# A two-layer attention and SiLU kernel: later raw loads for thirteen weight pairs, a token norm on ScalarE, one subtraction for two

## The chip, the cores and the metric

The kernel runs on one core of a Trainium2 chip. The time is device microseconds of one execution, the median of several. PE stands for TensorE's matmuls, PEld for its weight loads, DVE for VectorE, ACT for ScalarE, POOL for GpSimd, SP for SyncE (DMA issues and transposes). All times of the trace come from one profiled execution.

## The reference

The input x is 2048 tokens of width D = 576, in fp32.

```
for layer in (1, 2):
    x = x + attention(layernorm(x), wqkv) @ wo      # 32 heads of 18, a token looks at 8 tokens, 2 apart, backwards
    x = x + silu(layernorm(x) @ w1) @ w2            # w1: 576 x 4608, w2: 4608 x 576
```

Both layers use the same weights. layernorm has no scale or shift: (x − mean) / sqrt(var + 1e-5).

## The kernel before, in words

The tokens are cut into four chunks of 512 (four tiles of 128 tokens each), and the work into eight stages s = 0 to 7, two layers of four chunks. In each stage a chunk goes through attention, `project(s)` (the product with wo and the addition to x), a norm, and the hidden layer with w1 and w2. fp32 accuracy comes from fp16: each operand is split into a high part (x in fp16) and a low part (what is left), and a product is three fp16 products.

**Order.** Nobody writes the order of the instructions by hand. Each step is declared with `op(engine, cost, function, reads, writes, priority, after=...)`, and a planner (`Plan.order`) simulates the engines with these costs and the slots of the buffers, and hands out, for each engine, a fixed order. `after` names steps that must be over first. A new wait or a new cost therefore moves steps on all engines from that place on. Each engine works through its list strictly in order.

**Hidden layer.** Stages 0 and 1 multiply plainly (`ffn`, first products L1385, second products L1345). Stages 2 to 7 (`ffn_pairs`) take two of the 36 blocks of w1's columns together, a pair q = 0 to 17, and need seven products instead of eight (P1 to P7, L1232). For these, w1 must be brought into seven sums and differences, split into high and low. `prepare(q)` (L1064 to L1106) does so for each pair: eight raw loads on POOL's queue (L1072 four times 128 KB, L1076 four times 64 KB) into one of two `wr` slots, four sums on DVE (L1083), high parts on ACT (L1091), low parts on DVE (L1098, four per pair), and two stores on POOL (L1103) to `wfs` in HBM. `load_wf` (L1108) fetches them on SP. All 18 `prepare` are declared behind stage 0, and run beside stages 0 to 2. L1353 evicts second products of the pairs.

**Projection.** `project(s)` makes, for each of four token tiles, the high part of the attention's output (`yh`, L898 on DVE) and the low part (L492), lets SP turn the tile by a DMA transpose (L509, `yo<-yh`; `yh` has two slots), multiplies it by wo on PE in two halves (L925, 14 matmuls each, into one of three PSUM banks misc and z, which L1385 and L1232 use too), and adds the halves to x on DVE (L927). The list `flipped` collects the transposes. The third chunk's projection is the one at 555 to 600 us, beside the hidden layer of stage 1. POOL also fetches keys, values and queries for the attention (`kvs`, L779, 1584 KB; `qts`, L781, 288 KB).

**Norm and forms.** `forms` (L1158 on) takes bn_stats of a stage's x, `newton` (L524) finds r = 1/sqrt(var + eps), four L1179 on DVE write (x − mean) · r, L1184 makes differences of these, and L1193 (ACT) and L1198 (DVE) split them; L1203 turns them. Six stages use it. In stages 6 and 7 `hidden_forms` (L1283) makes four forms of the hidden h for the second product too: h4 = h6 + h3, h5 = h4 − h0, h2 = h1 − h5, h6 = h0 − h6.

Of the kernel before, what the change touches and what calls it, by code (L numbers as in the profile page):

```python
# [13 lines left out]
AF = mybir.ActivationFunctionType  # L14
ALU = mybir.AluOpType
AX = mybir.AxisListType

P = 128
# [8 lines left out]
NJ = 4  # L27
# [14 lines left out]
NP = NFT // 2  # L42
# [4 lines left out]
W2N = 11  # L47
FAR = 6
PREP = 0.9
PS = 0.45  # L50
S2 = 2
TWICE = {6: 0, 7: 0}
# [227 lines left out]
def sliding_attention_silu_ffn(ctx: ExitStack, tc: tile.TileContext, x, wqkv, wo, w1, w2, out):  # L280
# [243 lines left out]
    def newton(st, mv, nt, on_act, unit, js=slice(0, NJ)):  # L524

        v, r, a, b = (T(nt)[:, i, js] for i in (0, 1, 3, 4))
        if on_act == 2:
            nc.vector.tensor_scalar(v, T(st)[:, js, 0, 1], 1.0 / D, EPS, op0=ALU.mult, op1=ALU.add)
        else:
            nc.vector.tensor_scalar(v, T(mv)[:, js, 1], EPS, None, op0=ALU.add)  # L530
        nc.vector.tensor_scalar(a.bitcast(I32), v.bitcast(I32), 1, None, op0=ALU.logical_shift_right)
        nc.vector.tensor_scalar(r.bitcast(I32), a.bitcast(I32), -1, 0x5F3759DF, op0=ALU.mult, op1=ALU.add)
        for s in (1.0, unit):

            nc.vector.tensor_tensor(a, r, r, op=ALU.mult)
            nc.vector.tensor_tensor(a, a, v, op=ALU.mult)
            nc.vector.tensor_scalar(b, a, 0.375 * s, -1.25 * s, op0=ALU.mult, op1=ALU.add)
            nc.vector.tensor_tensor(b, b, a, op=ALU.mult)
            nc.vector.scalar_tensor_tensor(r, b, 1.875 * s, r, op0=ALU.add, op1=ALU.mult)
        if on_act in (1, 3):  # L540
            nc.vector.tensor_scalar(T(nt)[:, 2, js], T(mv)[:, js, 0], -1.0, None, op0=ALU.mult)

# [518 lines left out]
            nc.vector.tensor_scalar(dz, r12.rearrange("p (q f) i -> p q f i", f=2)[:, :, 0, 0], 2.0 / LNX, None, op0=ALU.mult)  # L1061
        op("DVE", 1.0, fn, [("s12", f) for f in range(NFT)] + [("sh", 2, g) for g in range(len(G2))], ["wsc"], -0.5)

    def prepare(q, prio):  # L1064

        w, v = Buf("wr"), Buf("ws")

        def load():
            t = T(w)
            for h in range(2):  # L1070
                for k in range(2):
                    nc.gpsimd.dma_start(t[:, h:4:2, k, :], w1[h * KH + k * P:h * KH + (k + 1) * P, 2 * q * P:(2 * q + 2) * P].rearrange(  # L1072
                        "p (f c) -> p f c", f=2))
                for f in range(2):
                    v = w1[h * KH + 2 * P:(h + 1) * KH, (2 * q + f) * P:(2 * q + f + 1) * P]
                    nc.gpsimd.dma_start(t[:, h + 2 * f, 2, :], bass.AP(tensor=v.tensor, offset=v.offset, ap=[[0, 4], *v.ap]))  # L1076
        op("POOL", 4.8, load, ["wsc"], [w], prio, nbytes=P * 12 * P * 4, lanes=8)

        def sums():
            t, u = T(w), T(v)  # L1080
            for o, a, b, f in ((u[:, 0], t[:, 2], t[:, 3], ALU.add), (u[:, 1], u[:, 0], t[:, 0], ALU.subtract),
                               (t[:, 2], t[:, 0], t[:, 2], ALU.subtract), (u[:, 2], t[:, 1], u[:, 1], ALU.subtract)):
                nc.vector.tensor_tensor(o, a, b, op=f)  # L1083
        op("DVE", 2.0, sums, [w], [w, v], prio)
        for x, r0, r1, g in ((w, 0, 4, Buf("wg")), (v, 4, 7, Buf("wh"))):
            n = r1 - r0

            def hi(x=x, g=g):
                d, t = T(g), T(x)
                for k0, k1, c in ((0, 2, 0), (2, 3, 1)):  # L1090
                    nc.scalar.activation(d[:, :, k0:k1, :].rearrange("p a b c -> p a (b c)"),  # L1091
                                         t[:, :, k0:k1, :].rearrange("p a b c -> p a (b c)"), AF.Copy, scale=wsc[:, q, c:c + 1])
            op("ACT", 0.4 * n, hi, [x, "wsc"], [(g, 0)], prio)

            def lo(x=x, g=g):
                d, t = T(g), T(x)
                for o, k0, k1 in ((3, 0, 2), (2, 2, 3)):
                    nc.vector.scalar_tensor_tensor(  # L1098
                        d[:, :, o:o + k1 - k0, :].rearrange("p a b c -> p a (b c)"),
                        t[:, :, k0:k1, :].rearrange("p a b c -> p a (b c)"), wsc[:, q, 0:1],  # L1100
                        d[:, :, k0:k1, :].rearrange("p a b c -> p a (b c)"), op0=ALU.mult, op1=ALU.subtract)
            op("DVE", 0.43 * n, lo, [x, (g, 0)], [(g, 0)], prio)
            op("POOL", 0.57, lambda g=g, r0=r0, r1=r1: nc.gpsimd.dma_start(  # L1103
                wfs[q][:, r0 * KB:r1 * KB], T(g).rearrange("p i a b -> p (i a b)")), [(g, 0)], [("wfs", q, r0 // 4)], prio, nbytes=P * n * KB * 2)
# [51 lines left out]
    def forms(xs, prio, home=None, late=(), into=None):  # L1156

        st, mv, nt = Buf("st"), Buf("mv"), Buf("nt")  # L1158
        for j in range(NJ):
            def stats(j=j):  # L1160
                for h in range(2):
                    nc.vector.bn_stats(T(st)[:, j, h, :], T(xs[j])[:, h * KH:(h + 1) * KH])
                nc.vector.bn_aggr(T(mv)[:, j, :], T(st)[:, j])
            op("DVE", 0.99, stats, [xs[j]], [(st, j), (mv, j)], prio)
        op("DVE", 2.55, lambda: newton(st, mv, nt, False, LNX), [(st, j) for j in range(NJ)] + [(mv, j) for j in range(NJ)], [nt], prio)
        out, ys = {}, [Buf(home[0]), Buf(home[1])] if home else [Buf(into)] * 2

        def view(a, r):
            if home:
                return T(ys[a])[:, r]  # L1170
            if r > 3:
                return T(ys[a])[:, a, r - 4]
            return T(xs[a + 2 - r // 2 * 2])[:, r % 2 * KH:(r % 2 + 1) * KH]

        def key(a, r):
            return (ys[a], r) if home else (ys[a], a, r) if r > 3 else xs[a + 2 - r // 2 * 2]
        for a in range(2):
            for j, r in ((a + 2, 0), (a, 2)):
                op("DVE", 0.58, lambda a=a, j=j, r=r: nc.vector.tensor_scalar(  # L1179
                    T(ys[a])[:, r:r + 2, :].rearrange("p a b -> p (a b)") if home else T(xs[j]), T(xs[j]), T(mv)[:, j, 0:1], T(nt)[:, 1, j:j + 1],  # L1180
                    op0=ALU.subtract, op1=ALU.mult), [xs[j], (mv, j), nt], [key(a, r), key(a, r + 1)], prio)

            for o, u, v in ((4, 0, 2), (5, 1, 4), (6, 1, 0), (7, 3, 5)):
                op("DVE", 0.45, lambda a=a, o=o, u=u, v=v: nc.vector.tensor_tensor(view(a, o), view(a, u), view(a, v), op=ALU.subtract),  # L1184
                   [key(a, u), key(a, v)], [key(a, o)], prio, after=late)
        for n in P_ORDER:
            r, x = Y_ROW[n], Buf("xf")
            for a in range(2):
                f = Buf("yf")

                def hi(f=f, a=a, r=r):
                    d, y = T(f), view(a, r)
                    nc.scalar.activation(d[:, 0:KH], y, AF.Copy)  # L1193
                    nc.scalar.activation(d[:, KH:KH + 32], y[:, 2 * P:KH], AF.Copy)

                def lo(f=f, a=a, r=r):
                    d, y = T(f), view(a, r)
                    nc.vector.tensor_tensor(d[:, 3 * P:KB], y[:, 0:2 * P], d[:, 0:2 * P], op=ALU.subtract)  # L1198
                    nc.vector.tensor_tensor(d[:, KH + 32:3 * P].rearrange("p (a b) -> p a b", a=2), y[:, None, 2 * P:KH].to_broadcast([P, 2, 32]),
                                            d[:, None, 2 * P:KH].to_broadcast([P, 2, 32]), op=ALU.subtract)  # L1200
                op("ACT", 0.65, hi, [key(a, r)], [(f, 0)] if home else [(f, 0), (x, "hold", a)], prio)
                done = op("DVE", 0.64, lo, [key(a, r), (f, 0)], [(f, 1)], prio)
                op("SP", 1.34, lambda f=f, a=a, x=x: nc.sync.dma_start_transpose(T(x)[:, :, a * P:(a + 1) * P], T(f)),  # L1203
                   [(f, 0), (f, 1)], [(x, a)], prio, nbytes=P * KB * 4)
            out[n] = x
        formed.append(done)
        return out
# [74 lines left out]

    def hidden_forms(q, hq, h, pd):  # L1283

        for r, u, v, o in ((4, 6, 3, ALU.add), (5, 4, 0, ALU.subtract), (2, 1, 5, ALU.subtract), (6, 0, 6, ALU.subtract)):
            op("DVE", 0.42, lambda hq=hq, r=r, u=u, v=v, o=o: nc.vector.tensor_tensor(T(hq)[:, r], T(hq)[:, u], T(hq)[:, v], op=o),
               [(hq, u), (hq, v)], [(hq, r)], pd - 0.01)
        for r0, r1, sh in ((0, 3, shx), (3, 7, shy)):
            sc = sh[:, q:q + 1]
            m = (r1 - r0) * 2 * P  # L1290
# [243 lines left out]
    for s in range(NL * NC):  # L1534
# [3 lines left out]
        else:  # L1538
            ffn_pairs(s, XT[s], X[s], TWICE.get(s, len(G2)))
        if s == 0:  # L1540
            for q in range(NP):
                prepare(q, PREP)
        if s == 2:
            op("POOL", 0.55, lambda: nc.gpsimd.dma_start(wos, fl(T(WO))), [(WO, k) for k in range(10)], ["wos"], 2.0, nbytes=P * 20 * D, after=flipped[-1:])
# [1 line left out]
            layer_norm(X[s], AN[s + NC] + 0.0, None, False, own=True, keep=xn[s - 2])  # L1546
        if s < NC - 1:
            front(s + 1)
        if s == NC - 1:
            norm(NC)  # L1550
            attend(NC)
# [41 lines left out]
```

## Time and profile before

| | |
|---|---|
| median of 3 runs | 2123.3 us (2121.58 to 2124.65) |
| the profiled execution | 2119.38 us, span 2117.6 us |
| PE busy | 2088.3 us (99%), 16017 matmuls |
| DVE busy | 1754.9 us (83%) |
| ACT busy | 1025.8 us (48%) |
| POOL busy | 388.5 us (18%) |
| chain of waits | PE 87%, DVE 6%, DMA 4% |

The span is from the first to the last instruction; the execution has 1.8 us around it. "Busy" leaves out DMA issues on SP and semaphores. The chain of waits is followed back from the last instruction, at each step to what released it.

### The profile page before, as it was taken

Reading aid. Unit: us, or ns where it says so; the run is one execution under the profiler, and the core shown is the slowest. Engines: PE = TensorE matmul, PEld = TensorE weight load, DVE = VectorE, ACT = ScalarE, POOL = GpSimd, SP = SyncE. Lnnn points to the kernel's source line nnn. Section 1 sums busy time; section 2 is a strip of 40 time slices with the busy share of each in tenths; the row PEclk is TensorE's granted clock in tenths of the full one; section 3 lists DMA queues with packets and bytes.
Section 4 is the critical chain, followed back from the end, with each engine's and each line's share of the span. In section 5 each row is a group of like instructions: output and inputs, shape, how many; then the busy total and the mean of one; then the engine's idle time right before and its main releaser. Section 6 shows DMA issues by size and latency. Waiting matters only on the chain.

```text
span 2117.6 us, 41751 instructions
## 1 busy us (share of the span) xinstructions
PE 2088.3 (99%) x16017; PEld 1539.5 (73%) x16017; DVE 1754.9 (83%) x2861; ACT 1025.8 (48%) x1857; POOL 388.5 (18%) x628
## 2 busy tenths in 40 slices
PE   8999999999999999999999999999999999999999
PEld 4556556665566888877786777777788888888887
DVE  8899999999876998679997978986996748766665
ACT  7555787644345454434434433434444545444442
POOL 2133566343322232011111001001000000000000
PEclk9999999999999999999999999999999999999999
DMA  6477777687989889886677896786989999779772
GB/s 188 146 212 256 236 258 248 214 243 221 250 206 297 264 275 252 210 261 189 177 220 208 218 273 195 217 225 185 247 256 302 330 258 290 218 213 272 221 210 76
DMA packets 377632, 489.07 MB, mean 231 GB/s; under 512 B 150600, under 2 KB 300724, under 8 KB 373080
## 3 DMA queue, kind: packets, MB, share of 16 engines
q1 hardware_dynamic: 332456, 336.85, 56.9%
q0 software_dynamic: 42960, 148.45, 21.8%
q8 instruction: 125, 2.05, 0.4%
q10 hardware_dynamic: 2016, 1.11, 0.2%
q14 instruction: 75, 0.61, 0.1%
HBM read 350.96 MB, written 86.85 MB: 207 GB/s over the span
## 4 chain that ended last, share of the span: by engine, by line
PE 87%; DVE 6%; DMA 4%; ACT 1%; issue 1%; SPq 0%; POOL 0%; ACTq 0%; DVEq 0%
PE acc L1345 19%; PE z L1232 16%; PE misc L1232 10%; PE z L735 9%; PE acc L1322 9%; PE z L1385 7%; PE acc L1409 4%; PE misc L1345 4%; PE misc L735 3%; PE z L925 3%; PE misc L1385 2%; PE misc L925 1%; DMA kvs<-kvs 1%; DMA yo<-yh 1%; DVE prs L837 1%
## 5 line engine op out<-in xcount | busy, mean ns | idle before, releaser
L1232 PEld LDWEIGHTS <-w 128*128 128x128 f16 x5292 | 516.5, 98 | 74.5 <-issue 2.5
L1345 PE MATMUL acc<-w,h 128*128 128x320 f16 (+2 forms) x3780 | 548.2, 280 | 2.3 <-DVE x L1353 2.3
L1345 PEld LDWEIGHTS <-h 128*128 128x128 f16 x4320 | 407.6, 98 | 122.3 <-issue 3.3
L1232 PE MATMUL z<-xb,w 128*128 128x256 f16 x3213 | 405.0, 273 | 0.5 <-DVE wq L1239 0.5
L1232 PE MATMUL misc<-xb,w 128*128 128x256 f16 x2079 | 272.2, 273 | 1.1 <-DVE wq L1239 0.8
L735 PEld LDWEIGHTS <-xa 128*128 128x128 f16 x1344 | 130.8, 98 | 115.5 <-issue 6.7
L837 DVE TENSOR_TENSOR prs<-qts,kvs 128x2304 f32<-128x2304 f32 x64 | 163.4, 2554 | 18.8 <-DMA kvs<-kvs 17.0
L870 DVE TENSOR_TENSOR prs<-kvs,pe 128x1152 f32<-128x1152 f32 x128 | 170.3, 1352 | 1.0
L841 DVE TENSOR_REDUCE lg<-prs 128x128 f32<-128x2304 f32 x64 | 163.1, 2548 | 0.9
L735 PE MATMUL z<-wq,xa 128*128 128x432 f16 x840 | 160.2, 346 | 2.1 <-ACT h L748 2.1
L1345 PE MATMUL misc<-w,h 128*128 128x384 f16 x540 | 139.7, 326 | 0.0
L877 DVE TENSOR_TENSOR prs<-prs 128x1152 f32<-128x1152 f32 (+1 forms) x128 | 135.1, 1056 | 3.2
L1331 DVE SCALAR_TENSOR_TENSOR x<-acc,d2x,x 128x576 f32<-128x576 f32 (+1 forms) x85 | 68.7, 810 | 57.2 <-PE acc L1322 56.6
L1385 PEld LDWEIGHTS <-w 128*128 128x128 f16 x588 | 57.9, 99 | 74.2 <-issue 7.6
L1409 PE MATMUL acc<-w,h 128*128 128x288 f16 x864 | 108.4, 286 | 1.9 <-DVE h L1392 1.1
L1409 PEld LDWEIGHTS <-h 128*128 128x128 f16 x864 | 83.7, 98 | 25.2 <-DVE h L1392 1.4
L1385 PE MATMUL z<-xb,w 128*128 128x512 f16 x420 | 93.9, 379 | 0.7 <-DVE w L1011 0.6
L1385 PE MATMUL z<-xb,wq 128*128 128x512 f16 x420 | 92.8, 379 | 1.7 <-ACT h L1387 1.7
L1236 ACT ACTIVATE wq<-z 128x256 f32<-128x256 f32 x107 | 40.8, 382 | 103.8 <-PE z L1232 103.7
L1387 ACT ACTIVATE h<-z,d 128x512 f32<-128x512 f32 x60 | 40.9, 682 | 94.9 <-PE z L1385 86.4
L1322 PEld LDWEIGHTS <-h 128*128 128x128 f16 x756 | 74.0, 98 | 17.6
L925 PEld LDWEIGHTS <-yo 128*128 128x128 f16 x672 | 65.7, 98 | 18.6 <-issue 1.9
(322 smaller groups left out, 3369.0 us busy)
## 6 DMA issues: line engine op xcount, KB each, us to landing
w<-wfs SPq DMA_DIRECT2D x756, 160.0 KB, 3.9
w<-w2s SPq DMA_DIRECT2D x180, 288.0 KB, 4.9
wq<-wqs SPq DMA_DIRECT2D x17, 1080.0 KB, 6.6
kvs<-kd POOLq DMA_DIRECT2D x8, 1584.0 KB, 8.4
w<-w1s SPq DMA_DIRECT2D x36, 320.0 KB, 5.9
wfs<-xa POOLq DMA_DIRECT2D x18, 640.0 KB, 4.6
kvs<-wts SPq DMA_DIRECT2D x80, 144.0 KB, 3.1
w2s<-w POOLq DMA_DIRECT2D x36, 288.0 KB, 4.7
```

The source lines that it names most:

```text
L735: nc.tensor.matmul(T(m)[:, :3 * UC], a, b, start=n == 0, stop=n == len(pl) - 1)
L837: nc.vector.tensor_tensor(T(pr), T(qt)[:, j:j + 2, None, :].to_broadcast([P, 2, W, UC]), win(T(kv), j, 2), op=ALU.mult)
L841: nc.vector.tensor_reduce(T(lg)[:, j:j + 2].rearrange("p a w h -> p (a w h)"), T(pr).rearrange("p a w (h d) -> p (a w h) d", d=DH), axis=A ...
L870: nc.vector.tensor_tensor(T(pr)[:, a].rearrange("p w (h d) -> p w h d", d=DH), v, T(pe)[:, j + a, :, :, None].to_broadcast([P, W, UH, DH]) ...
L877: nc.vector.tensor_tensor(t[:, :, 0:h, :], t[:, :, 0:h, :], t[:, :, h:2 * h, :], op=ALU.add)
L925: nc.tensor.matmul(T(m)[:, 0:288], a, b, start=n == 0, stop=n == len(pl) - 1)
L1232: nc.tensor.matmul(t, w[:, u, :], v[:, r, :], start=first and m == 0, stop=m == 6, skip_group_check=True)
L1322: nc.tensor.matmul(T(acc)[:, j, 0:KH], T(hb[t])[:, a, row[k], j * P:(j + 1) * P], T(wb[k, t])[:, w, :], start=k in (5, 1, 2) and t == 0 an ...
L1331: nc.vector.scalar_tensor_tensor(v, T(acc)[:, a:b, 0:KH], d2x[:, g:g + 1], v, op0=ALU.mult, op1=ALU.add)
L1345: nc.tensor.matmul(T(fa[b])[:, o:o + 2 * n].rearrange("p (a b) -> p a b", a=2), h(f, a, j), w(f)[:, :, v, c:c + n], start=q == f == m == 0 ...
L1385: nc.tensor.matmul(T(z), v, u, start=m == 0, stop=m == len(pl) - 1)
L1409: nc.tensor.matmul(T(acc)[:, h, 0:288], T(hb[q])[:, a, j * P:(j + 1) * P], T(wbs[q][0])[:, h, w, :], start=q == 0 and m == 0, stop=q == n ...
```

## The change

1. `prepare` of pairs 5 to 17 (HELD = 5 and on) is declared later, behind the third chunk's attention and projection, and its raw loads wait for the last entry of `flipped`, which is the transpose of the fourth tile of that projection.
2. In `forms`, the four normalisations of a stage go from DVE to ACT, as an Identity activation with scale r and bias −mean · r.
3. For these, `newton` gets one more 128x4 DVE operation (−mean · r), six times in all.
4. In `hidden_forms`, h5 = h4 − h0 and h6 = h0 − h6 become one DVE operation of 512 columns; the order is h4, then these, then h2.

```diff
+HELD = 5
...
+        if on_act == 4:
+            nc.vector.scalar_tensor_tensor(T(nt)[:, 2, js], T(mv)[:, js, 0], -1.0, r, op0=ALU.mult, op1=ALU.mult)
...
-    def prepare(q, prio):
+    def prepare(q, prio, after=()):
...
-        op("POOL", 4.8, load, ["wsc"], [w], prio, nbytes=P * 12 * P * 4, lanes=8)
+        op("POOL", 4.8, load, ["wsc"], [w], prio, nbytes=P * 12 * P * 4, lanes=8, after=after)
...
-        op("DVE", 2.55, lambda: newton(st, mv, nt, False, LNX), [(st, j) for j in range(NJ)] + [(mv, j) for j in range(NJ)], [nt], prio)
+        op("DVE", 2.55, lambda: newton(st, mv, nt, 4, LNX), [(st, j) for j in range(NJ)] + [(mv, j) for j in range(NJ)], [nt], prio)
...
-                op("DVE", 0.58, lambda a=a, j=j, r=r: nc.vector.tensor_scalar(
-                    T(ys[a])[:, r:r + 2, :].rearrange("p a b -> p (a b)") if home else T(xs[j]), T(xs[j]), T(mv)[:, j, 0:1], T(nt)[:, 1, j:j + 1],
-                    op0=ALU.subtract, op1=ALU.mult), [xs[j], (mv, j), nt], [key(a, r), key(a, r + 1)], prio)
+                op("ACT", 0.7, lambda a=a, j=j, r=r: nc.scalar.activation(
+                    T(ys[a])[:, r:r + 2, :].rearrange("p a b -> p (a b)") if home else T(xs[j]), T(xs[j]), AF.Identity,
+                    bias=T(nt)[:, 2, j:j + 1], scale=T(nt)[:, 1, j:j + 1]), [xs[j], (mv, j), nt], [key(a, r), key(a, r + 1)], prio)
...
-        for r, u, v, o in ((4, 6, 3, ALU.add), (5, 4, 0, ALU.subtract), (2, 1, 5, ALU.subtract), (6, 0, 6, ALU.subtract)):
-            op("DVE", 0.42, lambda hq=hq, r=r, u=u, v=v, o=o: nc.vector.tensor_tensor(T(hq)[:, r], T(hq)[:, u], T(hq)[:, v], op=o),
-               [(hq, u), (hq, v)], [(hq, r)], pd - 0.01)
+        op("DVE", 0.42, lambda: nc.vector.tensor_tensor(T(hq)[:, 4], T(hq)[:, 6], T(hq)[:, 3], op=ALU.add),
+           [(hq, 6), (hq, 3)], [(hq, 4)], pd - 0.01)
+
+        def differences():
+            t = T(hq)
+            first = bass.AP(tensor=t.tensor, offset=t[:, 4].offset, ap=[t.ap[0], [-4 * 2 * P, 2], [1, 2 * P]])
+            nc.vector.tensor_tensor(t[:, 5:7], first, t[:, 0:7:6], op=ALU.subtract)
+        op("DVE", 0.69, differences, [(hq, 4), (hq, 0), (hq, 6)], [(hq, 5), (hq, 6)], pd - 0.01)
+        op("DVE", 0.42, lambda: nc.vector.tensor_tensor(T(hq)[:, 2], T(hq)[:, 1], T(hq)[:, 5], op=ALU.subtract),
+           [(hq, 1), (hq, 5)], [(hq, 2)], pd - 0.01)
...
         if s == 0:
-            for q in range(NP):
+            for q in range(HELD):
                 prepare(q, PREP)
...
         if s < NC - 1:
             front(s + 1)
+        if s == 1:
+            for q in range(HELD, NP):
+                prepare(q, PREP, flipped[-1:])
```

The planner places everything anew from about 536 us on. The lines of the changed kernel are 3 higher up to L1284 (10 and more behind it).

SP's order around the third chunk's transposes, before. w_70 and w_87 are w1 and w2 blocks of stage 1's hidden layer, a pair of them per block.

```order
L941 DMA w_70<-w1s_166 128x1280
L509 DMA_TRANSPOSE yo<-yh 128x9x128
L946 DMA w_87<-w2s_199 128x1152
L941 DMA w_70<-w1s_167 128x1280
L509 DMA_TRANSPOSE yo<-yh 128x9x128 x2
L946 DMA w_87<-w2s_200 128x1152
L941 DMA w_70<-w1s_168 128x1280
L509 DMA_TRANSPOSE yo<-yh 128x9x128
```

And of the changed kernel:

```order
L944 DMA w_70<-w1s_164 128x1280
L510 DMA_TRANSPOSE yo<-yh 128x9x128 x2
L949 DMA w_87<-w2s_197 128x1152
L944 DMA w_70<-w1s_165 128x1280
L949 DMA w_87<-w2s_198 128x1152
L944 DMA w_70<-w1s_166 128x1280
L949 DMA w_87<-w2s_199 128x1152
L944 DMA w_70<-w1s_167 128x1280
L510 DMA_TRANSPOSE yo<-yh 128x9x128 x2
```

The first two transposes now go out together, two blocks earlier, and the last two together, three blocks behind them.

POOL's order at the same place, before. The raw loads (L1072, L1076) behind the second kvs fetch are those of pairs 6 and 7; wfs_219 to wfs_221 are the stores of pairs 5, 6 and 7.

```order
L1103 DMA wfs_219<-xa 128x2560
L1103 DMA wfs_219<-xa 128x1920
L779 DMA kvs<-kd_276 128x3168
L781 DMA qts<-qd_268 128x576
L1072 DMA wq<-in_B_w_dram 128x2x128 x2
L1076 DMA wq<-in_B_w_dram 128x1x128 x2
...
L1103 DMA wfs_220<-xa 128x2560
L1103 DMA wfs_220<-xa 128x1920
L1544 DMA wosd<-wos 128x5760
L1103 DMA wfs_221<-xa 128x2560
```

And of the changed kernel, in which the first loads behind the fetch are those of pairs 5 and 6, and wait for the fourth tile's transpose:

```order
L1106 DMA wfs_218<-xa 128x2560
L1106 DMA wfs_218<-xa 128x1920
L782 DMA kvs<-kd_276 128x3168
L784 DMA qts<-qd_268 128x576
L1075 DMA wq<-in_B_w_dram 128x2x128 x2
L1079 DMA wq<-in_B_w_dram 128x1x128 x2
...
L1106 DMA wfs_219<-xa 128x2560
L1106 DMA wfs_219<-xa 128x1920
L1554 DMA wosd<-wos 128x5760
L1106 DMA wfs_220<-xa 128x2560
```

POOL's work stands in the same order, one pair later, with the fetch of kvs and qts still ahead of the loads.

VectorE's order from the third of the projection's yh tiles on, before:

```order
L898 TENSOR_SCALAR yh<-o,so 128x576
L492 SCALAR_TENSOR_TENSOR yh<-o,so,yh 128x512
L492 SCALAR_TENSOR_TENSOR yh<-o,so,yh 128x64
L841 TENSOR_REDUCE lg_80<-prs 128x128
L898 TENSOR_SCALAR yh<-o,so 128x576
L927 SCALAR_TENSOR_TENSOR x_73<-misc_96,so,x_73 128x288
L492 SCALAR_TENSOR_TENSOR yh<-o,so,yh 128x512
```

And of the changed kernel:

```order
L901 TENSOR_SCALAR yh<-o,so 128x576
L493 SCALAR_TENSOR_TENSOR yh<-o,so,yh 128x512
L493 SCALAR_TENSOR_TENSOR yh<-o,so,yh 128x64
L901 TENSOR_SCALAR yh<-o,so 128x576
L493 SCALAR_TENSOR_TENSOR yh<-o,so,yh 128x512
L493 SCALAR_TENSOR_TENSOR yh<-o,so,yh 128x64
L844 TENSOR_REDUCE lg_80<-prs 128x128
L930 SCALAR_TENSOR_TENSOR x_73<-misc_96,so,x_73 128x288
```

The first eviction of the projection (L927, now L930) stands behind the fourth tile's yh in both; the fourth yh has moved up to the third.

## Rows read from the trace of the kernel before

**Rows 1.** The page, busy time of each engine with its share of the span and its number of instructions.
```profile
PE 2088.3 (99%) x16017; PEld 1539.5 (73%) x16017; DVE 1754.9 (83%) x2861; ACT 1025.8 (48%) x1857; POOL 388.5 (18%) x628
```
**Rows 2.** The waits of PE over the whole span, the first of the list: who waited for what, us in total, times, longest.
```profile
PE misc L1385 <- DVE x L927: 4.4, 1, 4.4
```
**Rows 3.** The waits of PE from 600 us to the end, all of the list; same columns.
```profile
PE acc L1345 <- DVE x L1353: 2.3, 5, 0.7
PE misc L925 <- DVE wq L1239: 1.8, 1, 1.8
PE misc L1232 <- DVE wq L1239: 0.8, 2, 0.5
PE z L1232 <- DVE wq L1239: 0.5, 1, 0.5
```
**Rows 4.** The chain of waits between 560 and 591 us: start, duration, what.
```profile
562.23 16.19 DMA yo<-yh
...
579.44 5.36 PE misc L1385 x14
...
588.24 3.02 PE misc L1385 x14
```
**Rows 5.** The timeline of DVE: start, duration (of all of a row together), engine, line, operation, tiles, count, and in brackets the idle time ahead and what ended it.
```profile
536.60 2.08 DVE L1083 TENSOR_TENSOR wq<-wq 128x384 f32<-128x384 f32 x4
...
544.87 3.40 DVE L1098 SCALAR_TENSOR_TENSOR xa<-wq,accw,xa 128x1024 f16<-128x1024 f32 x4
...
568.97 0.68 DVE L898 TENSOR_SCALAR yh<-o,so 128x576 f16<-128x576 f32 x1
...
578.44 0.52 DVE L898 TENSOR_SCALAR yh<-o,so 128x576 f16<-128x576 f32 x1 [5.35 <-DMA yo<-yh]
```
**Rows 6.** Windows: stretch, its length, busy time (and instructions) of PE, PEld, DVE, ACT and POOL, the granted clock as a share of full speed, the DMA engines' mean busy share, GB/s.
```profile
547.60:559.70 12.10, 12.10 (x58) 5.48 (x57) 11.93 (x17) 4.23 (x6) 5.99 (x10) 1.00 0.82 301
559.70:574.80 15.10, 15.10 (x125) 11.68 (x124) 13.28 (x11) 2.69 (x3) 7.21 (x10) 1.00 1.10 220
574.80:579.40 4.60, 0.26 (x3) 0.07 (x1) 0.96 (x3) 0.00 (x0) 0.00 (x0) 0.75 1.10 132
579.40:584.80 5.40, 5.36 (x16) 2.00 (x16) 5.23 (x13) 1.70 (x2) 0.00 (x0) 0.58 0.34 89
```
**Rows 7.** The timeline of SP's queue: transposes of the third and of the fourth chunk's projection; columns as in rows 5.
```profile
558.68 2.19 SPq L509 DMA_TRANSPOSE yo<-yh  x1
...
562.23 14.15 SPq L509 DMA_TRANSPOSE yo<-yh  x2
...
816.35 1.64 SPq L509 DMA_TRANSPOSE yo<-yh  x1
```
**Rows 8.** The timeline of POOL: the kvs fetch, the first and the last raw load of pairs 6 and 7, the first store of pair 6 and the last store of pair 17; columns as in rows 5.
```profile
554.21 0.54 POOL L779 DMA_DIRECT2D kvs<-kd  x1 [5.10 <-DVE prs L870]
...
555.27 1.43 POOL L1072 DMA_DIRECT2D wq<-in_B_w_dram  x2
...
573.80 0.70 POOL L1076 DMA_DIRECT2D wq<-in_B_w_dram  x1 [1.03 <-DMA wq<-in_B_w_dram]
591.87 0.58 POOL L1103 DMA_DIRECT2D wfs<-xa  x1 [17.36 <-DVE xa L1098]
...
845.94 0.54 POOL L1103 DMA_DIRECT2D wfs<-xa  x1 [4.25 <-DVE xa L1098]
```
**Rows 9.** The line L509 (all transposes of attention and projection): who waited for it (us, times), and the time from issue to landing.
```profile
  DVE yh L898: 5.4, 1
...
DMA to landing us min/median/max: 3.3/4.9/13.1
```
**Rows 10.** The timeline of PE: the first half of tile 0 of the fourth chunk's projection, the first product of pair 16 in stage 2 and that of pair 17; columns as in rows 5.
```profile
828.19 1.88 PE L925 MATMUL misc<-wos,yo 128*128 128x288 f16 x14
...
869.54 0.93 PE L1232 MATMUL misc<-xb,w 128*128 128x256 f16 x7
...
880.84 0.93 PE L1232 MATMUL z<-xb,w 128*128 128x256 f16 x7
```
**Rows 11.** The page's DMA issues: tiles, engine, count, KB each, median us from issue to landing.
```profile
w<-wfs SPq DMA_DIRECT2D x756, 160.0 KB, 3.9
...
kvs<-kd POOLq DMA_DIRECT2D x8, 1584.0 KB, 8.4
...
wfs<-xa POOLq DMA_DIRECT2D x18, 640.0 KB, 4.6
```
**Rows 12.** Groups of instructions by line over the whole span: line, engine, operation, tiles, shapes, count, busy us, mean ns of one, idle time ahead and what ended it. 16 of the 24 L1179 stand here, the other 8 have a mean of 578 to 602.
```profile
L1286 DVE TENSOR_TENSOR wq<-wq 128x256 f32<-128x256 f32 x96 | 38.6, 421 | 15.0 <-ACT wq L1261 10.2 <-ACT wq L1256 3.7
...
L591 ACT ACTIVATE yo<-x,nt 128x576 f32<-128x576 f32 x14 | 10.6, 767 | 4.1 <-DVE nt L541 2.3 <-DVE yh L492 1.6
L1179 DVE TENSOR_SCALAR x<-x,mv,nt 128x576 f32<-128x576 f32 x16 | 8.4, 574 | 0.0
...
L539 DVE SCALAR_TENSOR_TENSOR nt<-nt 128x4 f32<-128x4 f32 (+1 forms) x34 | 5.5, 162 | 1.2
```
**Rows 13.** Windows behind 600 us; columns as in rows 6.
```profile
600.00:860.00 260.00, 259.54 (x2063) 197.83 (x2061) 216.43 (x344) 124.06 (x215) 76.10 (x112) 1.00 0.90 262
860.00:1600.00 740.00, 735.80 (x5809) 559.30 (x5807) 632.27 (x974) 301.37 (x588) 72.03 (x124) 1.00 0.80 220
1600.00:2118.00 518.00, 512.54 (x4425) 430.48 (x4423) 345.61 (x633) 237.56 (x431) 12.90 (x24) 1.00 0.80 239
```

## The prediction

> **What bounds the kernel now.** I read the page first [rows 1]: PE is busy 99% of the span, VectorE 83%, ScalarE 48%. With PE that full, and the same 16017 matmuls after the change, a change of order can only give what PE loses by standing still or by running at a lower clock. So the second view is the list of PE's waits: one wait of 4.4 us is released by VectorE's L927, the longest single one of the run [rows 2]; after 600 us all waits together are 5.4 us [rows 3]. The third is the chain of waits around the long one [rows 4]. PE's first half of a hidden tile (L1385) waits for L927, the eviction of the third chunk's first projected half, because it needs that bank. L927 is ready long before, but on VectorE it stands behind the yh of the fourth tile (L898), which waits for one of the two yh slots, that is for a transpose (yo<-yh) which took 16.19 us. VectorE's rows show the same: its L898 at 578.44 has 5.35 us of idle ahead of it, put down to the transposed tile [rows 5].
>
> After the stop comes a second loss. The windows show the granted clock at 1.00 ahead of the stop, at 0.75 in the 4.6 us with it and at 0.58 in the 5.4 us behind it [rows 6], that is mostly the lower of TensorE's two levels, 1.2 and 2.4 GHz. Fourteen L1385 matmuls took 5.36 us behind the stop and 3.02 a little later [rows 4].
>
> Why was the transpose slow? SP issued the first tile's at 558.68 and the second and third at 562.23 [rows 7]. POOL issued a kvs fetch at 554.21, a qts fetch behind it, and then from 555.27 to 573.80 the sixteen raw loads of pairs 6 and 7, 1.5 MB [rows 8]. The windows have the DMA share between 0.82 and 1.10 over all of that [rows 6]. Over the whole run a transpose of this line lands in 3.3 to 13.1 us, median 4.9 (that view counts less of the issue than the chain's 16.19), and only here does anybody wait for one [rows 9].
>
> **Part 1, the wait for the turned tiles.** Pairs 5 to 17 can load only when the fourth tile of the third chunk's projection has been transposed. Pair 5, loaded well ahead of it before, moves behind it too. Two things follow at 555 to 580. No raw load runs beside the four transposes, and VectorE has pair 5's four sums (2.08) and four lows (3.40), 5.5 us together, no longer ahead of the yh tiles [rows 5]. So the transposes are issued some 6 us earlier. Walking through VectorE's new order with the durations of the old, I put tile 0's at about 552.6 (558.68 before; besides the 5.5, two L1392 now stand behind it) and tile 1's at about 554.1. In PE's new order tiles 0 and 1 stand together, 6 us earlier in PE's work; the first is needed at about 565.5, the second at 569, and the bank that the first half's eviction frees for tile 1's last half at 570.75. VectorE needs tile 0's yh slot at about 564.5 and tile 1's at 566: 11.9 us of room for each. At the median landing of 4.9 nobody waits. Bounds: 3.3 below, 16.2 above; with 16.2 the second tile lands at 570.3, 4.3 too late, and the stop is back. I take the low side, because the first tile of before, issued 4.5 us behind the kvs fetch and with five raw loads already out, had landed when VectorE reused its slot at 568.97, at most 10.3 us after its issue [rows 5, 7], and 10.3 fits into 11.9.
> What that gives: the stop 4.4 [rows 2] plus the slow matmuls 5.36 − 3.02 = 2.3 [rows 4], **6.7 us**. What it can lose: behind POOL's waiting loads stand later pairs' stores, the one of wos and, far later, the next kvs fetch; no reader of these is near. The pairs themselves come later. The last one was stored at 845.94 before [rows 8], and PE used it from 880.84 [rows 10]. In VectorE's new order its lows stand behind the evictions (L1353) of 11.25 pairs of the hidden loop, where 10.5 stood ahead before, and a pair lasts 11.3 us (from 869.54 to 880.84) [rows 10]: 8.5 us later, stored at about 854, landed 4.6 us on [rows 11]. That is 22 us ahead of PE, less 3.9 for the fetch [rows 11]. Cost 0; the cover is these 18 us, and its loss is rival 3.
>
> **Part 2, normalisation on ScalarE.** 24 instructions of some 0.576 (0.574 in the largest group [rows 12]) leave VectorE, 13.8 us; 24 activations come to ScalarE, for which L591, an activation of the same shape with its bias taken from a tile, is the nearest row: 0.767 each, 18.4 us [rows 12]. ScalarE is 48% busy in 600 to 860, 41% in 860 to 1600 and 46% behind it [rows 13], so this is hidden. The six small operations (-mean times r, 128x4) cost VectorE 6 x 0.16, from the 128x4 operations of L539 [rows 12], 1.0 us. Net 12.8 us off VectorE, which is 83 to 85% busy between 600 and 1600. But PE is busy 259.54 of 260 and 735.80 of 740 there [rows 13], and its waits behind 600 are 5.4 us in total [rows 3]: that is the most that a freer VectorE could give. It could also lose as much, since everything from about 536 us on is planned anew and these short waits, up to 1.8 each, depend on neighbours. I take 0. The norm's result now passes from ScalarE back to VectorE's differences, a handover more per tile; no PE wait in the list is released by the turned forms, so it costs nothing.
>
> **Part 3, one difference instead of two.** 36 times two L1286 of 256 columns, 0.421 each, become one of 512. A 4-column operation takes 0.162 [rows 12], so 256 columns more cost about 0.421 − 0.162 = 0.26 and 512 come to 0.68, against 0.84: 0.16 x 36 = 5.8 us of VectorE. In that stretch VectorE is 67% busy and PE 512.54 of 518, with some 4 us of the rest behind the last matmul [rows 13]. Taken as 0, between −1 and +1.
>
> **Sum.** The profiled execution took 2119.38 us, span 2117.6; less 6.7 it would be 2112.7. That execution stands 3.9 below the median of the three runs, 2123.3, which spread over 3.1 us. The stop's cause is the order of the program, so I take the same 6.7 off the median: **2116.6 us**, with 2113 to 2119 for the small waits in part 2. A measurement of this kernel tells some 0.2% from no change: under 2119.1 is faster, over 2127.5 slower.
>
> **Rivals.**
> 1. *The same wait, somewhere else* (same). The raw loads of the last pair are issued in the new order just ahead of tile 0 of the fourth chunk's projection, before some 5 us earlier. There the transpose went out at 816.35 [rows 7] and PE used it at 828.19 [rows 10], 11.8 us of room. If it takes 16.2 as the one at 562 did, it is 4.4 late, and 2.3 go to the clock: 6.7 lost, 2123. For it: the DMA share is 0.90 between 600 and 860 [rows 13]. Against it: it is one pair, not two, with no kvs fetch behind it.
> 2. *The change does not reach the cause* (same). The kvs and qts fetch, 1.87 MB, more than the raw loads of two pairs, still stand ahead of the transposes in POOL's new order, and the DMA share was 0.82 before the raw loads had started in earnest [rows 6]. If the fetch alone makes the second tile late, 16.2 from 554.1 gives 570.3, 4.3 late, and with the clock 6.6: 2123. Against it: the first tile's 10.3 at most. The kvs fetch lands in 8.4 us at the median [rows 11], and in the new order it is issued some 5 us earlier too, so it is over before 560.
> The Trainium skill, "DMA: Bandwidth & Descriptors", section Queues, rings and completion order, has each DMA engine take turns between the queues that have work, a packet from each; by that, how many loads wait in POOL's one queue would not matter, only whether any does, and rival 2 is how it would show. No row of the kernel before has these four transposes without POOL's transfers beside them, so the trace does not decide it.
> 3. *The pairs don't catch up* (slower). Twelve pairs went from the first load at 555.27 to the last store at 845.94, 24.2 us each [rows 8]. Thirteen now start at about 573. At the old pace the last store goes out at 888 and lands at 893, where its weights must be stored 3.9 us (a fetch of them [rows 11]) ahead of 880.84: PE stops 16 us, and with 2.3 for the clock and 6.7 gained the time is 2135. It decides at 23 us per pair, (872 − 573) / 13. For it: VectorE is 83% busy there [rows 13]. Against it: VectorE set the old pace (POOL waited 17.36 us for pair 6's lows ahead of its store at 591.87 [rows 8]), and its new order needs 21.6.
> 4. *VectorE's relief counts too* (faster). All 5.4 us of later waits go as well: 2111.
>
> **Chances.** Forecast 0.60, rival 1 0.15, rival 2 0.10, rival 3 0.08, rival 4 0.05, and 0.02 for a cost that no row shows, slower. Of the forecast I give 0.03 to times just above 2119.1. Faster 0.60 + 0.05 − 0.03 = 0.62, same 0.15 + 0.10 + 0.03 = 0.28, slower 0.10. The range runs from rival 4's 2111 to rivals 1 and 2 with the runs' spread, 2125.5, and leaves out rival 3; the forecast's own is 2113 to 2119.
>
> **What would show it.** In the profile after: no PE wait over 1 us between 540 and 600, yo<-yh not in the chain there, VectorE's L898 without an idle before it, raw loads from about 573, and a granted clock of 1.00 from 560 to 600. PE's busy time should fall by 2.3 and the PE idle by 4.4. It is wrong if the transposes issued near 553 land after 566, if a wait for yo<-yh shows at 820 to 850, or if an L1232 matmul near 885 waits for wfs.

## The result, and the profile after

The changed kernel took 2137.35 us (median of 5 runs, 2133.12 to 2141.83), beside 2121.58 of the kernel before (median of five runs; the 2123.3 that the prediction starts from is that of the first three): 1.0077 times as long, 95% interval 1.0054 to 1.0101. It is slower by 16 us where 6.7 us of gain were forecast, and outside the range. The profiled execution, the fastest of the five, has a span of 2131.3 us against 2117.6, 13.7 more. L492, L509, L898 and L1203 of the kernel before are L493, L510, L901 and L1206 here.

The waits of PE from 540 us on, the four longest; they answer to [rows 2, 3]:

```profile
PE misc L1355 <- ACT h L1399: 8.4, 1, 8.4
PE misc L1235 <- DMA xb<-yh: 4.0, 1, 4.0
PE misc L928 <- DVE x L930: 2.5, 1, 2.5
PE z L928 <- DMA yo<-yh: 1.6, 1, 1.6
```

The wait near 575 is still there (2.5 + 1.6 for 4.4), and two are new. The chain of waits shows what stands behind each of the three:

```profile
557.66 13.85 DMA yo<-yh
...
625.09 17.40 DMA xb<-yo
...
643.13 0.58 ACT h L1397
...
673.83 10.96 DMA xb<-yh
```

Each is a transpose that landed late: of the third chunk's projection (13.85 us), and twice of stage 2's forms (17.40 and 10.96). POOL's timeline, which answers to [rows 8], shows what ran beside them:

```profile
550.21 0.55 POOL L782 DMA_DIRECT2D kvs<-kd  x1 [12.59 <-DVE prs L873]
...
551.28 1.43 POOL L1075 DMA_DIRECT2D wq<-in_B_w_dram  x2
...
569.84 1.42 POOL L1079 DMA_DIRECT2D wq<-in_B_w_dram  x2 [4.31 <-DMA wq<-in_B_w_dram]
...
616.50 1.44 POOL L1075 DMA_DIRECT2D wq<-in_B_w_dram  x2
...
636.25 0.70 POOL L1079 DMA_DIRECT2D wq<-in_B_w_dram  x1 [4.57 <-DMA wq<-in_B_w_dram]
```

The first raw load of pair 5 went out at 551.28, as soon as POOL had issued the kvs and qts fetches. It waited for no turned tile. SP's timeline has the tiles' transposes only behind that first load, and forms' transposes in the middle of the loads of pairs 7 and 8 (616.50 to 636.25):

```profile
553.48 9.88 SPq L510 DMA_TRANSPOSE yo<-yh  x2
...
569.97 9.94 SPq L510 DMA_TRANSPOSE yo<-yh  x2
...
625.09 2.45 SPq L1206 DMA_TRANSPOSE xb<-yo  x1
...
631.04 5.26 SPq L1206 DMA_TRANSPOSE xb<-yo  x1
```

So the planner's `after` set the loads' place in POOL's list, where the plan had a pause ahead of them, and nothing on the chip made them wait. At the first place everything repeats what [rows 5] show, with pairs 5 and 6 in place of 6 and 7. VectorE's timeline:

```profile
571.54 0.52 DVE L901 TENSOR_SCALAR yh<-o,so 128x576 f16<-128x576 f32 x1 [5.21 <-DMA yo<-yh]
```

At the second place ScalarE is the engine in between. Its high parts of the forms (L1196) need slots that a transpose must free, and the hidden activations of stage 1 (L1397, L1399), for which PE waits, stand behind them in its list. ScalarE's timeline:

```profile
630.59 0.44 ACT L1196 ACTIVATE yh<-o 128x288 f16<-128x288 f32 x1 [5.61 <-DMA xb<-yh]
641.45 0.44 ACT L1196 ACTIVATE yh<-prs 128x288 f16<-128x288 f32 x1 [10.30 <-DMA xb<-yh]
...
643.04 0.67 ACT L1397 ACTIVATE h<-z,d 128x512 f32<-128x512 f32 x1
```

The windows (columns as in rows 6) show the clock behind the two new stops and what the DMA engines did:

```profile
616.50:625.00 8.50, 8.50 (x47) 4.27 (x46) 2.92 (x8) 5.58 (x12) 6.57 (x11) 1.00 0.99 265
625.00:636.00 11.00, 11.00 (x70) 6.51 (x68) 1.31 (x3) 0.56 (x2) 4.27 (x6) 1.00 1.11 137
636.00:644.50 8.50, 0.17 (x2) 0.00 (x0) 1.12 (x5) 2.42 (x6) 0.70 (x1) 0.69 1.15 171
644.50:655.00 10.50, 10.48 (x56) 6.49 (x57) 7.43 (x12) 4.95 (x8) 0.58 (x1) 0.76 0.48 170
...
674.00:685.00 11.00, 6.95 (x60) 5.40 (x58) 3.28 (x7) 2.64 (x8) 3.87 (x6) 0.94 1.19 192
685.00:692.00 7.00, 7.00 (x39) 5.03 (x39) 3.77 (x7) 1.48 (x4) 0.00 (x0) 0.61 1.17 212
```

The granted clock is 0.76 behind the stop near 640 and 0.61 behind that near 682. At full clock the work of the one would take 0.76 x 10.5 and of the other 0.61 x 7.0 us: 2.5 and 2.7 lost. From 625 to 636, while loads and transposes run beside each other, the DMA engines are busy (1.11) and move only 137 GB/s.

The loads at this place of the kernel before, there those of pairs 8 and 9, went out 5 us earlier, from 611.50, all of them ahead of the last four of stage 2's eight transposes (from 624.76 on). The DMA issues of this stretch (KB each, median us to landing), before, 605 to 640 us:

```profile
wq<-in_B_w_dram POOLq DMA_DIRECT2D x10, 128.0 KB, 5.5
```

and after, 610 to 645 us:

```profile
wq<-in_B_w_dram POOLq DMA_DIRECT2D x8, 128.0 KB, 10.7
```

Company alone does not make a transpose late. In the kernel before the loads ran beside forms' transposes too, with the DMA engines as busy, yet the two of these whose landing the trace tells took 6.2 and 7.7 us, and PE never stopped. Its window there:

```profile
625.00:636.00 11.00, 11.00 (x73) 6.83 (x72) 7.32 (x16) 6.70 (x13) 0.58 (x1) 1.00 1.22 215
```

Why a like company moves 215 GB/s there and 137 here is not shown. That the late transposes need the loads beside them is (e4, e6).

The account of the 13.7 us: near 575, 4.1 of waits and no low clock, where 6.7 were lost before (−2.6). New: 8.4 + 2.5 near 640 and 4.0 + 2.7 near 682 (+17.6). The short waits behind are 3.7 in place of 5.4 [rows 3] (−1.7). The sum is +13.3.

### The profile page after: what moved, and what is told of

Read it like the earlier page. It is cut to its first block, busy times and chain, and to the rows that moved or that the text cites. A ratio compares the mean times of both kernels' runs of the same rounds, so it can differ in the third digit from the quotient of the medians.

```text
span 2131.3 us, 41708 instructions
## 1 busy us (share of the span) xinstructions
PE 2091.4 (98%) x16017; PEld 1541.6 (72%) x16017; DVE 1741.0 (82%) x2807; ACT 1042.3 (49%) x1881; POOL 389.4 (18%) x628
## 3 DMA queue, kind: packets, MB, share of 16 engines
q10 hardware_dynamic: 2016, 1.11, 0.2%
## 4 chain that ended last, share of the span: by engine, by line
PE 86%; DVE 6%; DMA 5%; issue 1%; ACT 1%; POOL 1%; SPq 0%; ACTq 0%; DVEq 0%; POOLq 0%
PE acc L1355 20%; PE z L1235 16%; PE misc L1235 10%; PE acc L1332 8%; PE z L738 8%; PE z L1395 6%; PE misc L1355 4%; PE misc L738 3%; PE acc L1419 3%; PE z L928 2%; PE misc L1395 2%; PE misc L928 1%; DMA w<-in_B_w_dram 1%; DMA xb<-yo 1%; PE acc L916 1%
## 5 line engine op out<-in xcount | busy, mean ns | idle before, releaser
L1235 PE MATMUL misc<-xb,w 128*128 128x256 f16 x2037 | 266.6, 273 | 4.0 <-DMA xb<-yh 4.0
L738 PE MATMUL z<-wq,xa 128*128 128x432 f16 x812 | 154.3, 346 | 2.9 <-ACT h L751 2.9
L1332 PEld LDWEIGHTS <-h 128*128 128x128 f16 x756 | 74.0, 98 | 17.6
L1397 ACT ACTIVATE h<-z,d 128x512 f32<-128x512 f32 x60 | 40.9, 681 | 90.8 <-PE z L1395 85.8
```

The lines of the kernel that those rows point to most:

```text
L738: nc.tensor.matmul(T(m)[:, :3 * UC], a, b, start=n == 0, stop=n == len(pl) - 1)
L1235: nc.tensor.matmul(t, w[:, u, :], v[:, r, :], start=first and m == 0, stop=m == 6, skip_group_check=True)
L1332: nc.tensor.matmul(T(acc)[:, j, 0:KH], T(hb[t])[:, a, row[k], j * P:(j + 1) * P], T(wb[k, t])[:, w, :], start=k in (5, 1, 2) and t == 0 an ...
```

## The experiments

Ratios are to the kernel before, measured beside each, with 95% intervals; "site 1, 2, 3" are the stops near 575, 640 and 682.

| run | median us | ratio (interval) | PE waits at site 1, 2, 3, us |
|---|---|---|---|
| e1 edit 1 alone | 2136.13 | 1.0072 (1.0051, 1.0094) | 3.5, 6.2, 5.5 |
| e2 edits 2 to 4 | 2138.5 | 1.0087 (1.0070, 1.0104) | 6.0, 3.7, 0 |
| e3 one real wait | 2132.44 | 1.0059 (1.0040, 1.0079) | 0, 7.6, 6.3 |
| e4 all edits, loads of pairs 5 to 10 cut | 2112.37 | 0.9961 (0.9948, 0.9974) | 0, 0, 0 |
| e5 three real waits | 2127.77 | 1.0034 (1.0022, 1.0046) | 0, 0, 0 |
| e6 all edits, pairs 7 and 8 cut | 2126.34 | 1.0025 (1.0014, 1.0037) | 3.5, 0, 4.3 |
| e7 edit 1 alone, 5 to 10 cut | 2119.44 | 0.9991 (0.9980, 1.0003) | 0, 0, 0 |
| e8 before, pairs 6 and 7 cut | 2110.03 | 0.9955 (0.9939, 0.9971) | 0, 0, 0 |
| e9 before, pair 6 really waits | 2118.52 | 0.9990 (0.9980, 1.0000) | 0, 0, 2.1 |
| e10 e9 and edit 4 | 2117.4 | 0.9988 (0.9978, 0.9997) | 0, 1.7, 1.5 |
| e11 edits 2 to 4, pair 6 really waits | 2124.24 | 1.0016 (1.0004, 1.0028) | 0, 0, 3.3 |
| e12 edit 4 alone | 2120.86 | 1.0002 (0.9993, 1.0011) | 4.5, 0, 0 |
| e13 before, 5 to 10 cut | 2113.68 | 0.9964 (0.9951, 0.9977) | 0, 0, 0 |
| e14 edits 2 to 4, 5 to 10 cut | 2125.46 | 1.0022 (1.0011, 1.0034) | 0, 0, 0 |

**Which edit.** e1 is the kernel before with the HELD lines of the diff alone, e2 with all other lines.

> The kernel before with edit 1 alone (pairs 5 to 17 declared later, behind the third chunk's projection); norm and differences as before. Theory R: 'after' only moves the loads in POOL's order and puts no wait on the chip, so the raw loads of two pairs run beside the transposes of the third chunk's projection and again beside those of stage 2's forms. Then this edit alone carries the loss: 2128 to 2142 us, POOL's first raw load within 2 us of the kvs fetch near 551, PE waits of together over 8 us between 560 and 690, transposes landing over 12 us behind them. Rival N: the norm on ScalarE, and the high parts queued on ScalarE with stage 1's hidden activations, made the 8.4 us wait; then this kernel is within 5 us of the kernel before, 2117 to 2127, with no wait over 3 us between 600 and 690.

> The kernel before with edits 2, 3 and 4 (norm on ScalarE, -mean times r, one difference for two) and without edit 1. Theory R: loads stand where they stood, so the 4.4 us wait near 575 stays, none over 3 us comes between 600 and 690: 2115 to 2125 us. Rival N: the 8 us wait near 640 is here too, 2130 to 2138.

Edit 1 alone is as slow as all four (1.0072 beside 1.0077), its loads at 549.91 behind a kvs fetch at 548.83, and all three stops are there without any norm on ScalarE. But e2 is as slow by itself, above the ranges of both theories, so the losses of the edits do not add up: its plan has site 1 as before, longer (6.0), a stop of 3.7 near 640, and one of 6 us near 1045, to which e14 comes back. Rival N is out for edit 1, and not answered for e2.

**A wait that the chip has.** In e3, in front of pair 5's loads:

```diff
+            if touch:
+                nc.gpsimd.tensor_copy(t[:, 0, 0, 0:1], T(touch[0])[:, 0, 0:1])
...
-                prepare(q, PREP, flipped[-1:])
+                prepare(q, PREP, flipped[-1:], flat_tiles[-1] if q == HELD else None)
```

> The changed kernel with a wait that the chip really has: POOL copies one column of the fourth turned tile into the place of pair 5's first raw load ahead of the loads (it is overwritten by them). The order of all engines is that of the changed kernel but for this copy. Theory R: first raw load behind 566 instead of 551, the first two transposes land within 11 us, the PE waits near 570 to 576 (4.5 us together) go; the waits near 640 and 682 stay or move by a few us: 2128 to 2135 us. Rival K: the kvs fetch alone makes the transposes late; then they land as late as in the changed kernel (13.9 us) and the wait stays, 2135 to 2139.

POOL's timeline in e3, the copy and the first raw load:

```profile
574.98 0.18 POOL L1076 CAST wq<-yo 128x1 f32<-128x1 f16 x1 [25.36 <-DMA yo<-yh]
575.50 1.43 POOL L1079 DMA_DIRECT2D wq<-in_B_w_dram  x2 [0.34 <-POOL wq L1076]
```

SP's and VectorE's rows there: the first two transposes, and the yh that waited 5.21 us in the changed kernel.

```profile
551.79 7.85 SPq L510 DMA_TRANSPOSE yo<-yh  x2
```

```profile
564.56 0.51 DVE L902 TENSOR_SCALAR yh<-o,so 128x576 f16<-128x576 f32 x1
```

No engine waits at site 1 any more, PE's list of waits from 540 to 620 is empty, although the kvs fetch still stands ahead at 548.53. Rival K, my rival 2, falls: it takes the raw loads, not the fetch alone. The later stops stay, as expected, and with them most of the loss.

**The loads taken away.** e4, e6 and e8 skip seven of a pair's eight raw loads and change no order:

```diff
+                    if 5 <= q <= 10 and (h or k):
+                        continue
...
-                for f in range(2):
+                for f in range(0 if 5 <= q <= 10 else 2):
```

> The changed kernel, in which pairs 5 to 10 load one of their eight raw blocks (128 of 768 KB); the rest of their raw weights is left out, old data stands there. Orders unchanged but for the missing loads. Theory R: all three groups of waits (4.5 near 572, 8.4 near 640, 4.2 near 682) and the lower clock behind them go: 2112 to 2120 us. Rival N (ScalarE's order): the waits near 640 and 682 stay, 2130 to 2135.

> The changed kernel, in which only pairs 7 and 8 load one of their eight raw blocks; the rest of their raw weights is left out. Orders unchanged. Theory R: the wait of 8.4 us near 640 goes with the lower clock behind it, those near 572 (4.5) and 682 (4.2) stay: 2123 to 2130 us. Rival: if the wait near 640 came from pairs 5 and 6 having moved work there, it stays, 2135 to 2139.

> The kernel before, in which pairs 6 and 7 load one of their eight raw blocks (the rest of their raw weights is left out). Orders unchanged. My prediction's first term: the wait near 575 (4.4) and the slow matmuls behind it (2.3) go, 6.7 us: 2112 to 2117 us. Rival K: the kvs fetch alone keeps the second transpose late, 2119 to 2124.

All three stops go as theory R has it, though e8 came 2 us under its range. With the loads gone the changed kernel's order has no PE wait at all between 540 and 700 (e4). With only pairs 7 and 8 cut, site 2 alone goes (e6, waits from 540 to 800):

```profile
PE misc L1237 <- DMA xb<-yh: 4.3, 1, 4.3
PE misc L928 <- DVE x L930: 2.5, 1, 2.5
PE z L928 <- DMA yo<-yh: 1.0, 1, 1.0
```

and with pairs 6 and 7 cut in the kernel before (e8) its stop goes; the span is 2107.9, 9.7 us shorter. PE is busy without a gap from 560 to 600 there, at a granted clock of 1.00, so the 6.7 us of the stop and its slow matmuls are gone: my term stands, and so does its cause. The other 3 us I cannot place.

**All three kept apart.** e5 has e3's copy also in front of pair 7 (for stage 2's eighth turned form) and pair 9 (for the last):

```diff
-                prepare(q, PREP, flipped[-1:])
+                at = {HELD: flat_tiles[-1], HELD + 2: (XT[2][P_ORDER[3]], 1), HELD + 4: (XT[2][P_ORDER[6]], 1)}.get(q)
+                prepare(q, PREP, flipped[-1:], at)
```

> The changed kernel with three waits that the chip really has, each a POOL copy of one column of a turned tile into the place of a raw load: pair 5 for the fourth tile of the third chunk's projection, pair 7 for stage 2's eighth turned form, pair 9 for its last. The planner knows of them, so the order after 575 is planned anew. Theory R: no raw load runs beside a transpose that somebody waits for; no PE wait over 2 us between 560 and 690, 2110 to 2119 us. Rival P (any new plan after 550 brings waits of its own of some 10 us): 2125 to 2140, with PE waits at other places.

Both were half right. No PE wait is left between 540 and 690, but the loads come later, and stage 2's end pays. The longest of its waits from 845 to 930:

```profile
PE z L1239 <- DMA w<-wfs: 2.3, 2, 2.1
PE misc L1359 <- ACT h L1274: 1.7, 1, 1.7
PE z L1239 <- DVE wq L1246: 1.7, 1, 1.7
```

The chain there goes through a fetch of pair 16's weights, the sixth of seven issued in a burst from 871.44 on, and landing late:

```profile
873.76 8.43 DMA w<-wfs
```

That is a new wait in place of the old ones, near where my rival 3 had one. Pair 16's last store had gone out at 854.9, 16.5 us ahead of the burst, so the store was not what held it: SP's list has forms' transposes ahead of the burst, and it waited for their operands (8.5 us up to 860.9, 3.6 up to 868.2). Pair 17 is as rival 3 had it, on SP: its last store went out at 873.8, and SP waited 5.9 us, up to 882.0, for it to land. No wait of PE is put to pair 17's fetches.

**Only as much wait as needed.** e9 is the kernel before with pairs 6 on held for the second turned tile (`HELD = 6`, `flat_tiles[-3]`) by the copy; e10 adds edit 4, e11 edits 2 to 4.

> The kernel before with one wait that the chip really has, and no other edit: pair 6's raw loads (and so pair 7's behind them) wait, by a POOL copy of one column of a turned tile into the place of a raw block, for the second turned tile of the third chunk's projection. POOL's order is that of before. Theory R: the loads begin about 10 us later, the transposes land in time, the wait of 4.4 near 575 and the slow matmuls go, pairs 7 and on are hardly later, so no new wait over 2 us: 2112 to 2117 us. Rival P (every new plan brings waits of its own): 2119 to 2130.

> The run before with edit 4 (two differences as one) on top. By part 3 of the prediction 0 from the edit itself: within 3 us of the run before, 2111 to 2118 us; by rival P 2119 to 2130.

> Edits 2, 3 and 4, with the hold from pair 6 on and as a wait on the chip for the second turned tile (HELD = 6), in place of the planner's wait for the fourth from pair 5 on. Theory R: no wait near 572; whether pairs 7 to 10 meet the forms' transposes depends on the plan: if their loads begin more than 10 us ahead of them, 2110 to 2118 us, if beside them 2120 to 2132 with PE waits between 630 and 690. Rival N (ScalarE's norm costs by itself): 2125 or more with no transpose landing late.

e9's profiled execution has a span of 2112.0, and POOL's copy and load stand at:

```profile
568.55 0.19 POOL L1074 CAST wq<-yo 128x1 f32<-128x1 f16 x1 [14.70 <-DMA yo<-yh]
569.07 1.43 POOL L1077 DMA_DIRECT2D wq<-in_B_w_dram  x2 [0.34 <-POOL wq L1074]
```

Site 1 is gone, but a forms' transpose is late at 667 (2.1 us), and over ten runs (2113.78 to 2123.48) the median is 2118.52: the profiled execution is the fastest of them, and the gain that holds is 2 us (interval 0 to 4), of 5.6 in the profile. That lies between the ranges of theory R and of rival P. e10 is the best version that keeps all the work, 0.12% under the kernel before; its interval overlaps e9's. e11 cures site 1 as well and loses it again at 683 and 942.

**The edits by themselves.** e12 is edit 4 alone; e7, e13 and e14 complete a square with e4, all with the loads of pairs 5 to 10 cut.

> The kernel before with edit 4 alone; the orders differ only from stage 6's hidden forms on. Part 3 of the prediction: 0, between 1 us faster and 1 slower, 2118 to 2124 us, the new operation 0.68 us long. Rival P: 2125 or more by a wait of the new plan behind 1700.

> Edit 1 alone, with the raw loads of pairs 5 to 10 cut as in the run with all edits (the rest of these raw weights is left out). It differs from that run, 2112.4 us, by edits 2 to 4, with the collisions gone from both. My prediction's parts 2 and 3 say 0 for these edits: 2110 to 2115 us. If a freer VectorE is worth the 5 us of short waits, this is slower, 2116 to 2119; if the activations cost, it is faster, 2105 to 2109.

> The kernel before with the raw loads of pairs 5 to 10 cut to one block of eight (the rest of these raw weights is left out). By the run with pairs 6 and 7 cut (2110.0) the loads of 5 and 8 to 10 make nobody wait: 2109 to 2112 us.

> Edits 2 to 4 without edit 1, the same loads cut. Theory R (their loss of 17 us came from transposes that landed late beside raw loads near 580 and 640, and beside a load of wqs near 1030): the first two go, some 14 of the 17 us, the third stays: 2118 to 2126 us. Part 2 of the prediction (the edits by themselves 0) with no collision left: 2108 to 2114. Rival N (the norm on ScalarE costs by itself): 2130 or more.

Edit 4 alone is worth nothing, as forecast, and its operation takes 0.691 us. The square reads: no edit 2113.7, edit 1 2119.4, edits 2 to 4 2125.5, all 2112.4. Edits 2 to 4 are 12 us slower without edit 1 and 7 us faster with it, so no fixed price of theirs explains it. e7 missed its range by 4 us and e13 by 2. The three longest single waits of PE in e7 are for DMAs (2.6, 2.0 and 1.6 us, at 1214, 1206 and 951); e4 has none over 1.5. e14's list from 540 us on begins:

```profile
PE z L1236 <- DVE wq L1243: 6.2, 2, 5.9
PE misc L737 <- DVE wq L1243: 2.9, 1, 2.9
```

The longer stop ends at 1037, with a granted clock of 0.68 over the 7.9 us behind it, and the chain ahead of it goes through

```profile
1012.23 15.97 DMA xa<-yh
```

a transpose of layer 2's norm in another crowd of DMAs (a fetch of wqs, 1080 KB, and of weights on SP's own queue), with no raw load near. The shorter ends at 930, behind a DMA of 8.58 us (xn<-yh, issued at 918.48), with a clock of 0.69 over 9.6 us. The two stops and their clock make 2.9 + 3.0 + 5.9 + 2.5 = 14.3 of the 15.6 us by which e14's span (2127.5) is above e13's (2111.9), which has neither. So most of the 12 us is late DMAs in that plan; what edit 2 costs by itself stays open, and edits 2 and 3 were not run apart.

## Why the prediction was wrong, point by point

- **What bounds the kernel: right.** The stop near 575, the slow matmuls behind it and the raw loads as the cause: in e8 the stop and the low clock are gone.
- **Part 1, the wait: wrong, and this is the step that failed.** "Pairs 5 to 17 can load only when the fourth tile ... has been transposed" took the planner's `after` for a wait of the chip. The raw loads began at 551.28, not about 573, and the transposes, issued at 553.48 about where I had put them, met them. The order of POOL, quoted ahead of the prediction, showed the loads straight behind the kvs fetch; that nothing in the loads reads a turned tile can be read from `load()`, which touches `w1` and its own slot. The sentence on POOL's changed order that has these loads wait for the fourth tile's transpose is wrong for the same reason. With a real wait the mechanism works as predicted: the loads begin at 575.50 and nobody waits at site 1 (e3), with 11.4 us from the first issue at 551.79 to the third yh at 563.14.
- **Part 1, what it can lose: the second failure.** I looked for later pairs' readers (the stores, the fetches of pair 17) and costed the rest at nothing. The loads of pairs 7 to 10, a few us later against the forms, met those transposes: 17.6 us. This term weighs more than the missing wait: with the wait made real (e3) the kernel is still 0.6% slower. Pair 17's last store went out at 880.1, not about 854: 25.3 us a pair from the first load on, where I had 21.6. The 18 us of cover were gone; PE, itself 16 us later, did not wait for it.
- **Rival 1 had the mechanism at another place.** I set it at the fourth chunk's projection (816 to 828), where no stop came; it struck at stage 2's forms, whose transposes I had only checked for "no PE wait in the list", a list made with other neighbours. I gave it 6.7 us once; it came twice, at 10.9 and 6.7.
- **Rival 2 is out** by e3 and e8: the kvs fetch alone makes nobody wait. The Trainium skill, "DMA: Bandwidth & Descriptors", section Queues, rings and completion order, lets queues take turns; at site 1 the transposes were late only where raw loads gave POOL's queue work for longer, which that rule allows. These runs do not test the rule itself.
- **Part 2: the sizes were off a little, the sum stays open.** The activation with scale and bias took 0.856 us, not 0.767, 24 times; the small operation 0.161 as estimated. VectorE's busy time fell from 1754.9 to 1741.0, by 13.9 where parts 2 and 3 make 18.6; the difference stays open. The short waits behind 600, which I said were the most that relief could give or take, are dwarfed by what a new plan did (e2, e14).
- **Part 3: right**, 0.691 against 0.68 estimated, and 0 in time (e12).

## What to carry to other kernels

An order that a planner makes with a dependency of its own is not a dependency on the chip: before costing a wait, name the semaphore or the tile that enforces it. When bulk loads move, list every transpose and small transfer in their new neighbourhood with the room that each has, not only the one that was to be cured. And an edit that re-plans a list scheduler must be measured with its plan: here the same edits were worth −7 or +12 us (with the raw loads cut), depending on the plan around them.

## What the runs showed that was not expected

Where transposes landed late beside raw loads, the loads were late too: 10.7 us to land instead of 5.5, the DMA engines being busy 1.11 of the time for 137 GB/s. A like company in the kernel before, a few us earlier, moved 215 GB/s and cost PE no wait; what makes the difference is not shown. An in-order ScalarE then carried the lateness of a transpose of one stage to the matmuls of another (site 2). And a profiled execution can be the fastest of ten (e9: 2113.8 in a median of 2118.5), so an account of a profile is one of that execution.
